# Six durations in the cost model that orders the expert and dense stage

## The chip, the cores and the metric
The kernel runs on one core of a Trainium2 chip. The metric is the device time of one execution in microseconds (us); the kernel before has a median of 881.43 us over 3 runs (877.85 to 882.18 us).

## The reference, cut to what matters
Three parts follow one another. Windowed attention with 32 global tokens gives 2176 tokens of 512 features. A router then assigns each token to exactly one of 8 experts, 272 tokens each, in falling order of the logits, and each expert computes two layers on its tokens. A dense layer with a rational activation closes.

```python
logits = x @ w_gate                       # x: attention's output, 2176 x 512
for idx in np.argsort(-logits.flatten()): # greedy, at most cap = 272 tokens per expert
    ...
for e in range(8):                        # 512 -> 1024 -> 512
    out[mask] = np.maximum(x[mask] @ w1[e], 0.0) @ w2[e]
h = out @ w_in                            # 512 -> 2048
P = a[0] + a[1]*h + a[2]*h**2 + a[3]*h**3
Q = 1.0 + abs(b[0])*abs(h) + abs(b[1])*h**2
y = (P / (Q + 1e-6)) @ w_out              # 2048 -> 512
```

## The kernel before, in words
Attention takes the first 190 us and is ordered by a planner of its own; the diff does not touch it. The stage after it, called the expert and dense stage here, runs on one planner object (`Flow`) with several generators that work side by side:

- `router` goes through 8 phases (`phase`, line 1188). Each but the last has a search (`search`, from line 988): 7 VectorE steps on a 136-element table, then six rounds of a wide comparison on VectorE (L1015), 17 small products on TensorE (L1019), a reduction (L1023), a broadcast product (L1027) and two or three narrow VectorE steps. `members` then turns the choice into token numbers (`idx`, L1167).
- `gather` fetches the tokens of an expert by three indirect DMAs from GpSimd (L1416), transposes them on TensorE (L1443) and splits each value into a high and a low part (L1428, L1430). Expert 0's gather waits for a staging slot (`t1_s`) that the conversions of the last dense weights also use.
- `loads` and `splits` bring expert weights in and split them: the high part on ScalarE (L1480), the low part by a subtraction on GpSimd (L1489; for every second piece of expert 0 on VectorE).
- `experts` has both layers of each expert: 64 groups of 3 products of 272 columns (`mm3`, L1244 to L1246), in which high and low parts are multiplied crosswise.
- `firsts` is the first dense layer, in chunks of two experts' blocks of 128 tokens (256 columns; the last chunk 384), again with `mm3`. After each bank of 512 (or 384) values comes `chain`, the activation: five ScalarE steps (L1620, L1622, L1627, L1641, L1643) and seven VectorE steps (L1638, L1630, L1632, L1654, L1656, L1658, L1660). L1654 and L1660 give the high and the low part of the result. One such bank with its chain is called a dense step below.
- `seconds` is the second dense layer, 3 products of 512 columns per group (`mm3t`, L1249 to L1251); the first two need the high part, the third the low part.
- `high`, `last_pieces`, `low_pe` and `low` finish the dense weights while the router's first searches run: conversions from 64-bit words on VectorE (L265 to L267), high parts on ScalarE (L1234), low parts by correction products on TensorE (L1355, L1356), by a copy on ScalarE (L1361), or on VectorE (L1379).

What sets the order is `Flow.run` (line 158 on). A generator yields the pair (engine, planned duration) before it issues instructions, and events, slots or rings before things it must wait for. The planner keeps a planned clock for each engine, adds a lag between dependent steps (0.2 us across engines, 0.14 us on VectorE), and takes at each turn, among the steps of an engine that could start within its patience, the one with the lowest rank. The engines' queues are then written in that order (`manual_schedule`), and at run time each engine goes through its queue in order, waiting on semaphores alone. The planned durations therefore never reach the chip. They set the order, and through `fill` (line 1719) how many filler products are put into planned gaps of TensorE before expert 0:

```python
t, e, d = min((max([self.free(e)] + [t + self.lag(s, e) for t, s in p[2]]) + sum(less), e, d)
              for e, d, *less in p[3])
...
wait = patience.get(e, 0.0)
x = min((x for x in c if x[0] <= t0 + wait), key=lambda x: (x[1], x[0]))
```

Ranks follow progress: `experts` has 2 + its share of experts done, `firsts` 2 + chunks done, `seconds` 0.1 less; `router` has 0 in its first two phases and later 0.6 or 1.5, and from its third phase on waits another `LAG` = 0.5 us of planned time before each TensorE step.

Of the kernel before, what the change touches and what calls it, by code (L numbers as in the profile page):

```python
# [188 lines left out]
def moe_kernel(ctx: ExitStack, tc: tile.TileContext, q_l, k_l, v_l, q_g, k_g, v_g, w_gate, w1, w2,  # L189
# [998 lines left out]
    def phase(j):  # L1188
        if j < E - 1:
            found = yield from search()  # L1190
        else:
            est = rw.tile([128, E], F32, name="est")
            yield "DVE", 0.3
            V.tensor_scalar(est, OPEN, 0.0, None, op0=OP.is_gt)
            found = *chosen(est), rps(128, 2 * E + 4 * NT)
        il = yield from members(j, *found, j == E - 1)
        yield from note(j, il)
# [80 lines left out]
    front = {"e": -1.0, "d": 0.0, "r": 0.0, "open": False}  # L1278

    def mmt(cols, n=1):  # L1280
        return n * cols / 2400

    def wide(n):
        return mo.tile([128, 512], F32, name=n, bufs={"rows": NR, "p": 2}[n])
# [99 lines left out]
    def router():  # L1384
        for j in range(E):
            if j >= 3:
                yield started[j - 3]
            for n, item in enumerate(phase(j)):
                front["r"] = j + n / 76
                if j > 1 and isinstance(item, tuple) and item[0] == "PE":  # L1390
                    yield LAG
                yield item
# [73 lines left out]
    def splits():  # L1466
        for j in range(E):
            for i in range(NX):
                alt = j == 0 and i % 2 == 1
                yield raw_done[j][i]  # L1470
                yield t2_s if alt else w_s
                yield "ACT", 0.52
                raw = raws.pop((j, i))
                if alt:
                    t = mo.tile([128, 2, 4, 128], F32R, name="t2", bufs=2)
                    hi, lo = t[:, 0], t[:, 1]
                else:
                    hi = mo.tile([128, 4, 128], F32R, name="whi", bufs=2)
                    lo = mo.tile([128, 4, 128], F32R, name="wlo", bufs=2)
                nc.scalar.activation(hi, raw, AF.Copy)  # L1480

                def rest(j, i, alt, raw, hi, lo):
                    if j < 2:
                        yield sought[j]
                    if alt:
                        yield "DVE", 0.6
                    else:
                        yield "POOL", 1.23
                    (V if alt else nc.gpsimd).tensor_tensor(lo, raw, hi.bitcast(F32), op=OP.subtract)  # L1489
                    wparts[j, i] = hi, lo, t2_s if alt else w_s  # L1490
                    flow.fire(w_done[j][i])
                    flow.fire(rows_s)

                flow.go(rest(j, i, alt, raw, hi, lo), -0.1)

    def experts():

        for j in range(E):
# [5 lines left out]
            for f in range(FC):  # L1504
                yield w_done[j][f]
                yield sc_s
                whi, wlo, slots = wparts.pop((j, f))
                ph = None
                for k in range(KC):
                    if f == 0:  # L1510
                        yield x_done[j][k]
                    yield "PE", mmt(CAP, 3)
                    if k == 0:
                        ph = four.pop(0)
                    mm3(ph[:, :CAP], whi[:, k], wlo[:, k], xhi[:, k], xlo[:, k], k == 0, k == KC - 1)
                    front["open"] = k < KC - 1
                    front["e"] = j - 1 + ER * (f + (k + 1) / KC) / NX
                flow.fire(slots)

                def act(j, f, ph, hs):  # L1520
                    yield "ACT", 0.28
                    hh = mo.tile([128, CAP], F32R, name="hh", bufs=FC)
                    hl = mo.tile([128, CAP], F32R, name="hl", bufs=FC)
                    nc.scalar.activation(hh, ph[:, :CAP], AF.Relu)  # L1524
                    yield "DVE", 0.35
                    V.scalar_tensor_tensor(hl, ph[:, :CAP], 0.0, hh.bitcast(F32), op0=OP.max, op1=OP.subtract)
                    hs[f] = hh, hl
                    four.append(ph)
                    flow.fire(sc_s)
                    flow.fire(h_done[j][f])  # L1530

                flow.go(act(j, f, ph, hs), -0.2)
            flow.fire(layer1[j])
            for d in range(KC):
                yield sc_s
                py = None
                for g in range(FC // 4):
                    i = FC + d * (FC // 4) + g
                    yield w_done[j][i]
                    whi, wlo, slots = wparts.pop((j, i))  # L1540
                    for c in range(4):
                        f = 4 * g + c
                        yield h_done[j][f]
                        yield "PE", mmt(CAP, 3)
                        if f == 0:
                            py = four.pop(0)
                        mm3(py[:, :CAP], whi[:, c], wlo[:, c], *hs[f], f == 0, f == FC - 1)
                        front["open"] = f < FC - 1
                        front["e"] = j - 1 + ER * (i + (c + 1) / 4) / NX
                    flow.fire(slots)  # L1550
# [22 lines left out]
    def shape(c):  # L1573
        T = 128 * len(BLK[c])
        return T, 512 // T
# [29 lines left out]
    def chain(c, i, ph):  # L1605
        T, FW = shape(c)
        big = FW > 1
        u = FW * T / 512
        own = big or i % 3 < 2
        hold = [t1_s] if own else [rows_s] * 3  # L1610
        for x in hold:
            yield x
        yield "ACT", 0.57 * u
        if own:
            t1 = mo.tile([128, 2, 512], F32, name="t1", bufs=2)
            p, q, r = wide("p"), t1[:, 0], t1[:, 1]
        else:
            p, q, r = [wide("rows") for _ in range(3)]
        p, q, r = [x[:, :FW * T] for x in (p, q, r)]
        nc.scalar.activation(q, ph, AF.Abs, scale=b0)  # L1620
        yield "ACT", 0.48 * u
        nc.scalar.activation(r, ph, AF.Square)  # L1622
        numer, quad = Event(), Event()

        def numerator():
            yield "ACT", 0.66 * u
            nc.scalar.activation(p, ph, AF.Identity, scale=a_[3], bias=a_[2])  # L1627
            yield quad
            yield "DVE", 0.6 * u
            V.tensor_tensor(p, p, ph, op=OP.mult)  # L1630
            yield "DVE", 0.66 * u
            V.scalar_tensor_tensor(p, p, a_[1], ph, op0=OP.add, op1=OP.mult)  # L1632
            flow.fire(numer)
            flow.fire(tq_s)

        flow.go(numerator(), 1)
        yield "DVE", 0.66 * u
        V.scalar_tensor_tensor(q, r, b1, q, op0=OP.mult, op1=OP.add)  # L1638
        flow.fire(quad)
        yield "ACT", 0.61 * u  # L1640
        nc.scalar.activation(r, q, AF.Ln, bias=cq)  # L1641
        yield "ACT", 0.52 * u
        nc.scalar.activation(r, r, AF.Exp, scale=-1.0)  # L1643
        yield numer
        slots = t2_s if big or i % 2 else w_s
        yield slots

        yield "DVE", 0.66 * u
        if slots is t2_s:
            t2 = mo.tile([128, 2, 512], F32R, name="t2", bufs=2)  # L1650
            gh, gl = t2[:, 0, :FW * T], t2[:, 1, :FW * T]
        else:
            gh, gl = [mo.tile([128, 512], F32R, name=n, bufs=2)[:, :FW * T] for n in ("whi", "wlo")]
        V.scalar_tensor_tensor(gh, p, a_[0], r, op0=OP.add, op1=OP.mult)  # L1654
        yield "DVE", 0.66 * u
        V.scalar_tensor_tensor(q, q, cq, gh.bitcast(F32), op0=OP.add, op1=OP.mult)  # L1656
        yield "DVE", 0.66 * u
        V.scalar_tensor_tensor(q, p, a_[0], q, op0=OP.add, op1=OP.subtract)  # L1658
        yield "DVE", 0.6 * u
        V.tensor_tensor(gl, q, r, op=OP.mult)  # L1660
        gs[c, i] = gh, gl, slots
        for x in hold:
            flow.fire(x)
        flow.fire(g_done[c][i])
# [108 lines left out]
```

## Time and profile before

| | before |
|---|---|
| median of 3 runs | 881.43 us (877.85 to 882.18) |
| profiled execution, its own time | 881.8 us |
| its span | 880.0 us |
| mean granted TensorE clock | 0.973 |
| TensorE busy | 830.7 us (94%), 7945 products |
| VectorE busy | 712.1 us (81%) |
| ScalarE busy | 504.1 us (57%) |
| GpSimd busy | 260.8 us (30%) |
| first product of expert 0 starts | 248.4 us |
| last product starts | 873.5 us |

How to read it: all times inside a trace count from the start of the span. Engines are PE (TensorE products), PEld (its weight loads, which run beside products), DVE (VectorE), ACT (ScalarE), POOL (GpSimd) and SP (SyncE, which issues DMAs). L1244 is line 1244 of the kernel. A product's duration includes time in which the next one already runs, since products are pipelined; the spacing of their starts is the better measure of pace. The granted clock is a share of full speed (1.00 is 2.4 GHz, half of it 1.2 GHz).

### The profile page before, as it was taken

The numbers are of one execution on the slowest core, as the hardware profiler recorded it, in microseconds if no ns is written. First come the engines' busy times: TensorE is split into PE (matmuls) and PEld (weight loads), VectorE is DVE, ScalarE is ACT, GpSimd is POOL, SyncE is SP. The second block draws the span as 40 slices with busy tenths as digits, with TensorE's granted clock in tenths as the row PEclk, the third lists the DMA queues.
The fourth block names the chain that finished last, engine by engine and source line by source line (L and its number), as shares of the span: only waits on it lengthen the run. The fifth ranks groups of instructions, "written<-read, shape, count | busy, mean of one in ns | idle before, by whom it ended". The sixth has DMA issues, their size and how long they took to land.

```text
span 880.0 us, 20528 instructions
## 1 busy us (share of the span) xinstructions
PE 830.7 (94%) x7945; PEld 730.3 (83%) x7956; DVE 712.1 (81%) x1647; ACT 504.1 (57%) x1137; POOL 260.8 (30%) x227
## 2 busy tenths in 40 slices
PE   8887988879899999999999999999999999999997
PEld 5665766657689899999889999998999999998995
DVE  4557777758889989989998989999887767668985
ACT  4665676759544545545554554555455555556753
POOL 7510220000223334233442433334243343330001
PEclk9998997989999999999999999999999999999999
DMA  9989885623444222221331222133223122210000
GB/s 218 243 237 271 207 254 160 181 77 97 141 123 122 73 60 62 73 85 37 97 97 48 73 75 83 37 97 98 60 61 107 50 73 84 85 37 13 13 1 36
DMA packets 130538, 88.99 MB, mean 101 GB/s; under 512 B 28840, under 2 KB 119464, under 8 KB 130440
## 3 DMA queue, kind: packets, MB, share of 16 engines
q1 hardware_dynamic: 126632, 76.92, 31.6%
q0 software_dynamic: 3280, 10.75, 3.7%
q8 instruction: 62, 1.02, 0.5%
q14 instruction: 36, 0.29, 0.1%
q10 hardware_dynamic: 528, 0.02, 0.0%
HBM read 70.02 MB, written 8.92 MB: 90 GB/s over the span
## 4 chain that ended last, share of the span: by engine, by line
PE 65%; DVE 14%; issue 10%; DMA 6%; ACT 3%; SPq 2%; POOL 1%; DVEq 0%; POOLq 0%; ACTq 0%
PE sc L1244 6%; PE sc L1246 6%; PE sc L1245 5%; PE sc L1251 5%; PE sc L1249 5%; PE sc L1250 5%; PE tq L1244 5%; PE tq L1245 5%; PE tq L1246 5%; PE sc L596 3%; DMA stg<-in_moe_w_out_dram 2%; SPq L383 2%; PE sc L494 2%; PE tq L1355 2%; PE av L1019 2%
## 5 line engine op out<-in xcount | busy, mean ns | idle before, releaser
L1489 POOL TENSOR_TENSOR wlo<-rows,whi 128x512 fp32r<-128x512 f32 x120 | 168.0, 1402 | 333.3 <-ACT whi L1480 324.7
L1244 PE MATMUL tq<-yr,wh 128*128 128x256 f32 (+1 forms) x512 | 148.4, 290 | 1.5 <-DVE p L1632 1.5
L1245 PE MATMUL tq<-yr,wh 128*128 128x256 f32 (+1 forms) x512 | 147.4, 288 | 0.0
L1246 PE MATMUL tq<-yr,ws 128*128 128x256 f32 (+1 forms) x512 | 146.9, 287 | 0.0
L1249 PE MATMUL sc<-wh,t 128*128 128x512 f32 x248 | 99.9, 403 | 0.0
L1251 PE MATMUL sc<-wh,t 128*128 128x512 f32 x248 | 99.0, 399 | 0.8 <-DVE t L1660 0.7
L1244 PEld LDWEIGHTS tq<-yr,wh 128*128 128x128 f32 x512 | 96.5, 188 | 3.1 <-issue 2.2
L1250 PE MATMUL sc<-ws,t 128*128 128x512 f32 x248 | 97.9, 395 | 0.0
L1245 PEld LDWEIGHTS tq<-yr,wh 128*128 128x128 f32 x512 | 96.4, 188 | 0.8
L1246 PEld LDWEIGHTS tq<-yr,ws 128*128 128x128 f32 x512 | 96.6, 189 | 0.0
L1480 ACT ACTIVATE whi<-rows 128x512 fp32r<-128x512 f32 x120 | 75.1, 628 | 17.0 <-PE sc L1245 13.1
L1620 ACT ACTIVATE t<-tq,coef 128x512 f32<-128x512 f32 (+1 forms) x67 | 44.9, 670 | 52.5 <-PE tq L1246 40.9
L1524 ACT ACTIVATE hh<-sc 128x272 fp32r<-128x272 f32 x64 | 25.4, 397 | 86.4 <-PE sc L1246 86.1
L1244 PE MATMUL sc<-xhi,whi 128*128 128x272 f32 x240 | 72.9, 304 | 0.0
L1244 PE MATMUL sc<-hh,whi 128*128 128x272 f32 x240 | 70.6, 294 | 0.0
L1246 PE MATMUL sc<-xhi,wlo 128*128 128x272 f32 x240 | 69.6, 290 | 0.5 <-POOL wlo L1489 0.5
L1246 PE MATMUL sc<-hh,wlo 128*128 128x272 f32 x240 | 69.3, 289 | 0.0
L1245 PE MATMUL sc<-hl,whi 128*128 128x272 f32 x240 | 69.2, 288 | 0.0
L1245 PE MATMUL sc<-xlo,whi 128*128 128x272 f32 x240 | 69.1, 288 | 0.0
L1638 DVE SCALAR_TENSOR_TENSOR t<-t,b 128x512 f32<-128x512 f32 (+1 forms) x67 | 52.0, 776 | 20.3 <-ACT t L1622 20.2
L1641 ACT ACTIVATE t<-t,cq 128x512 f32<-128x512 f32 (+1 forms) x67 | 47.3, 706 | 23.4 <-DVE t L1638 23.2
L1251 PEld LDWEIGHTS sc<-wh,t 128*128 128x128 f32 x248 | 46.6, 188 | 15.9 <-DVE t L1660 5.2
(313 smaller groups left out, 2182.2 us busy)
## 6 DMA issues: line engine op xcount, KB each, us to landing
rows<-in_moe_w_dram SPq DMA_DIRECT2D x128, 256.0 KB, 2.8
stg<-in_moe_w_in_dram SPq DMA_DIRECT2D x16, 512.0 KB, 4.3
stg<-in_moe_w_out_dram SPq DMA_DIRECT2D x16, 512.0 KB, 7.8
VW<-vr SPq DMA_DIRECT2D x18, 256.0 KB, 3.2
kr<-in_k_l_dram SPq DMA_DIRECT2D x8, 512.0 KB, 5.9
qr<-in_q_l_dram SPq DMA_DIRECT2D x8, 512.0 KB
vr<-in_v_l_dram SPq DMA_DIRECT2D x16, 256.0 KB, 5.3
xd<-xs SPq DMA_DIRECT2D x64, 64.0 KB, 3.3
```

The lines of the kernel that those rows point to most:

```text
L596: nc.tensor.matmul(ps[64 * j:64 * j + 64, n * 128:(n + 1) * 128], qb_t[u // 2][:, 2 * hg + j, u % 2 * 4 + n].rearrange("p a q -> p (a q)") ...
L1244: nc.tensor.matmul(ps, whi, xhi, start=first, stop=False)
L1245: nc.tensor.matmul(ps, whi, xlo, start=False, stop=False)
L1246: nc.tensor.matmul(ps, wlo, xhi, start=False, stop=last)
L1249: nc.tensor.matmul(ps, ghi, whi, start=first, stop=False)
L1250: nc.tensor.matmul(ps, ghi, wlo, start=False, stop=False)
L1251: nc.tensor.matmul(ps, glo, whi, start=False, stop=last)
L1480: nc.scalar.activation(hi, raw, AF.Copy)
L1489: (V if alt else nc.gpsimd).tensor_tensor(lo, raw, hi.bitcast(F32), op=OP.subtract)
L1620: nc.scalar.activation(q, ph, AF.Abs, scale=b0)
L1638: V.scalar_tensor_tensor(q, r, b1, q, op0=OP.mult, op1=OP.add)
L1641: nc.scalar.activation(r, q, AF.Ln, bias=cq)
```

## The change
Six kinds of planned durations get other values: `mmt`, which prices the products of `experts`, `firsts` and `seconds`; every VectorE step of `router` (0.05 us more); the GpSimd subtraction of an expert weight; and five VectorE steps of `chain`. No instruction, buffer, slot, rank or patience is edited.

```diff
--- before.py
+++ after.py
@@ -1278,7 +1278,7 @@
     front = {"e": -1.0, "d": 0.0, "r": 0.0, "open": False}
 
     def mmt(cols, n=1):
-        return n * cols / 2400
+        return n * (cols / 2260 + 0.005)
 
     def wide(n):
         return mo.tile([128, 512], F32, name=n, bufs={"rows": NR, "p": 2}[n])
@@ -1387,6 +1387,8 @@
                 yield started[j - 3]
             for n, item in enumerate(phase(j)):
                 front["r"] = j + n / 76
+                if isinstance(item, tuple) and item[0] == "DVE":
+                    item = ("DVE", item[1] + 0.05)
                 if j > 1 and isinstance(item, tuple) and item[0] == "PE":
                     yield LAG
                 yield item
@@ -1485,7 +1487,7 @@
                     if alt:
                         yield "DVE", 0.6
                     else:
-                        yield "POOL", 1.23
+                        yield "POOL", 1.4
                     (V if alt else nc.gpsimd).tensor_tensor(lo, raw, hi.bitcast(F32), op=OP.subtract)
                     wparts[j, i] = hi, lo, t2_s if alt else w_s
                     flow.fire(w_done[j][i])
@@ -1634,7 +1636,7 @@
             flow.fire(tq_s)
 
         flow.go(numerator(), 1)
-        yield "DVE", 0.66 * u
+        yield "DVE", 0.7 * u
         V.scalar_tensor_tensor(q, r, b1, q, op0=OP.mult, op1=OP.add)
         flow.fire(quad)
         yield "ACT", 0.61 * u
@@ -1645,18 +1647,18 @@
         slots = t2_s if big or i % 2 else w_s
         yield slots
 
-        yield "DVE", 0.66 * u
+        yield "DVE", 0.72 * u
         if slots is t2_s:
             t2 = mo.tile([128, 2, 512], F32R, name="t2", bufs=2)
             gh, gl = t2[:, 0, :FW * T], t2[:, 1, :FW * T]
         else:
             gh, gl = [mo.tile([128, 512], F32R, name=n, bufs=2)[:, :FW * T] for n in ("whi", "wlo")]
         V.scalar_tensor_tensor(gh, p, a_[0], r, op0=OP.add, op1=OP.mult)
-        yield "DVE", 0.66 * u
+        yield "DVE", 0.76 * u
         V.scalar_tensor_tensor(q, q, cq, gh.bitcast(F32), op0=OP.add, op1=OP.mult)
-        yield "DVE", 0.66 * u
+        yield "DVE", 0.72 * u
         V.scalar_tensor_tensor(q, p, a_[0], q, op0=OP.add, op1=OP.subtract)
-        yield "DVE", 0.6 * u
+        yield "DVE", 0.78 * u
         V.tensor_tensor(gl, q, r, op=OP.mult)
         gs[c, i] = gh, gl, slots
         for x in hold:
```

## Rows read from the trace of the kernel before

**Rows 1.** Stretches: busy us of each engine (instructions), granted clock, DMA share, GB/s.
```profile
230.00:240.00 10.00, 6.97 (x63) 5.24 (x62) 7.94 (x22) 3.53 (x6) 5.53 (x5) 0.91 0.37 108
240.00:249.00 9.00, 7.94 (x80) 6.26 (x80) 6.08 (x24) 2.67 (x6) 0.00 (x0) 0.72 0.50 147
...
600.00:650.00 50.00, 49.96 (x393) 45.82 (x392) 44.78 (x104) 25.19 (x46) 20.25 (x18) 1.00 0.20 61
650.00:700.00 50.00, 49.56 (x365) 46.18 (x364) 37.95 (x62) 27.89 (x52) 20.02 (x17) 1.00 0.32 93
```
**Rows 2.** Timeline, TensorE: start us, duration us, line, operation, out<-in, shape, count.
```profile
502.84 0.28 PE L1246 MATMUL tq<-yr,ws 128*128 128x256 f32 x1
...
504.25 0.28 PE L1246 MATMUL tq<-yr,ws 128*128 128x256 f32 x1
...
507.49 0.40 PE L1249 MATMUL sc<-wh,t 128*128 128x512 f32 x1
...
508.65 0.39 PE L1251 MATMUL sc<-wh,t 128*128 128x512 f32 x1
```
**Rows 3.** TensorE's waits, 262 to 640 us: us in total, times, longest.
```profile
PE av L1027 <- DVE d L1023: 1.3, 2, 0.9
...
PE sc L1246 <- POOL wlo L1489: 0.5, 3, 0.2
PE av L1063 <- DVE aa L1058: 0.4, 1, 0.4
```
**Rows 4.** TensorE's waits, 640 to 880 us.
```profile
PE tq L1244 <- DVE p L1632: 1.5, 1, 1.5
PE sc L1251 <- DVE t L1660: 0.7, 3, 0.3
PE tx L1443 <- DMA rows<-xd,idx: 0.4, 1, 0.4
```
**Rows 5.** Groups by line and shape, 262 to 875 us: busy us, mean ns, idle before.
```profile
L1489 POOL TENSOR_TENSOR wlo<-rows,whi 128x512 fp32r<-128x512 f32 x114 | 160.0, 1405 | 314.5 <-ACT whi L1480 305.9 <-issue 6.0 <-PE tq L1246 2.5
...
L1660 DVE TENSOR_TENSOR t<-t 128x512 fp32r<-128x512 f32 x56 | 53.2, 950 | 0.6
...
L1638 DVE SCALAR_TENSOR_TENSOR t<-t,b 128x512 f32<-128x512 f32 x56 | 45.3, 808 | 18.8 <-ACT t L1622 18.7
...
L1620 ACT ACTIVATE t<-tq,coef 128x512 f32<-128x512 f32 x56 | 38.5, 687 | 41.7 <-PE tq L1246 37.7 <-DVE d L1023 3.0 <-PE av L1027 0.7
```
**Rows 6.** Timeline, a dense step whose last product waits (in brackets: idle before, releaser).
```profile
727.88 1.67 DVE L1660 TENSOR_TENSOR t<-t 128x512 fp32r<-128x512 f32 x1
...
729.60 0.50 PE L1251 MATMUL sc<-wh,t 128*128 128x512 f32 x1 [0.34 <-DVE t L1660]
```
**Rows 7.** Timelines of the lead-in by engine, and the landing line of the gather.
```profile
219.52 0.42 DVE L265 TENSOR_SCALAR p<-stg 128x512 int32<-128x512 int32 x1
...
222.73 0.30 DVE L996 TENSOR_REDUCE m<-wide_b 128x17 f32<-128x136 f32 x1
...
234.69 3.08 DVE L265 TENSOR_SCALAR p<-stg 128x512 int32<-128x512 int32 x1
...
234.01 0.95 POOL L1416 DMA_INDIRECT p<-xd,idx  x1 [0.82 <-ACT ws L1361]
234.98 2.49 POOL L1489 TENSOR_TENSOR wlo<-rows,whi 128x512 fp32r<-128x512 f32 x2
...
DMA to landing us min/median/max: 3.2/3.5/4.2
...
238.70 0.21 PE L1027 MATMUL av<-identb,d 128*128 128x32 bf16 x1 [2.65 <-DVE d L1023]
...
241.90 0.58 PE L1019 MATMUL av<-oh,wide_a 128*128 128x8 bf16 x17
...
244.28 0.58 PE L1019 MATMUL av<-oh,wide_a 128*128 128x8 bf16 x17 [0.68 <-DVE wide_a L1015]
...
245.18 0.67 PE L1443 MATMUL tx<-identf,t 128*128 128x128 f32 x2
```

## The prediction, made before the changed kernel was run

> **What bounds the kernel now.** I read the slices of the span first, then busy time by stretches, then who waits for whom on TensorE, then the timeline where TensorE stops. From about 250 us to 873.5 us TensorE is busy in 99 to 100% of nearly every stretch, at the full granted clock, while VectorE has 44.8 of 50 us while the router runs and 38.0 of 50 us once it has ended, about 660 us [rows 1]. A busy TensorE is not yet a TensorE at its peak, so I checked the spacing of starts. Between the starts at 502.84 and 504.25 us lie 12 intervals of 256 columns, 0.1175 us each; between 507.49 and 508.65 us lie 5 of 512 columns, 0.232 us each [rows 2]. Back to back, then. The code has 512 groups of three for the experts (272 columns), 512 for the first dense layer (448 of them with 256 columns and 64 with 384) and 272 for the second (512). With 0.1175 and 0.232 us read directly, and 0.125 and 0.175 us for 272 and 384 columns as estimates on the line through these two, that is 158 + 34 + 192 + 189 = 573 us of 625 us. The rest is the router's small products, the transposes of gathered rows, weight loads that these leave uncovered, and waits. The waits that the profile names from 262 us on are few: four kinds before 640 us, from 1.3 down to 0.4 us and 3.0 us in all [rows 3], of which the first, the third and the last stand there, and three after it, 1.5, 0.7 and 0.4 us [rows 4]. So 5.6 us is all that a better order could take from named waits in this stage. The other place is the lead-in, 191 to 248 us, where the first search of the router is a chain between VectorE and TensorE and TensorE has real holes: 6.97 busy us of 10 and 7.94 of 9 in its last two stretches, at granted clocks of 0.91 and 0.72 [rows 1].
>
> **The change part by part.** No instruction is added, removed or resized. Six numbers change in a model that only decides in which order each engine's queue is written. The chip's durations are what they were, so the cost is that of other neighbours in five queues and of a few filler products.
>
> *Products, cols/2400 to cols/2260 + 0.005.* 256 columns go from 0.1067 to 0.1183 us and 512 from 0.2133 to 0.2315 us; the chip's 0.1175 and 0.232 us [rows 2] agree with the new ones. Over 1,253,376 columns in 3,888 products the plan grows from 522 to 574 us, the chip by 0. What goes with it is a hidden margin: for each 10 us that TensorE really worked, the old plan counted about 9.1 us, so whatever was planned just in time came 0.9 us early.
>
> *Activation chain.* The five repriced VectorE steps were planned at 4 x 0.66 + 0.60 = 3.24 us, are now at 0.70 + 0.72 + 0.76 + 0.72 + 0.78 = 3.68 us, and took 4.35 us on average, from 0.808 us for the first of the five to 0.950 us for the last [rows 5]. The five ScalarE steps keep prices below their means, the first 0.57 against 0.687 us [rows 5]. A chain's plan is about 7.5 us long, so it loses 0.09 x 7.5 = 0.7 us of margin by the new products and gets 0.44 us back: 0.25 us less per dense step. TensorE already takes some steps the moment they end: at 729.60 us the third product of a step waited for the subtraction that had started at 727.88 us and took 1.67 us [rows 6].
>
> *Router steps, +0.05 us.* One of them is planned at 0.21 us and took 0.30 us [rows 7]. Up to about 661 us some nine of them run inside one chain on the same engine, which gives back 0.4 us of plan: the 0.25 us above are covered there. After 661 us that cover is gone. Some 17 dense steps lie between there and the last chunk. The price lies between 0 (the margin is not used) and 17 x 0.25 = 4.3 us; I take +1.0 us, near the lower end, since such waits are 0.7 us in all [rows 4]. The last chunk, after 799 us, is out of it: its steps are made well ahead of their use, and its one wait is for another step (1.5 us at L1244) [rows 4].
>
> *GpSimd subtraction, 1.23 to 1.40 us.* Its mean is 1.405 us [rows 5]. GpSimd idles 314 us of this stage, and TensorE waits for it 0.5 us in all [rows 3]. Between -0.5 and +0.5 us; I take 0. With the longer last step of the chain (0.60 to 0.78 us) the 0.7 us that L1251 waits can go in part: -0.7 to 0, I take -0.3 us.
>
> *Lead-in.* The last gathered rows of expert 0 are issued by 234.96 us and rows land 3.5 us after their issue in the median [rows 7], here at about 238.5 us; their first transpose starts at 245.18 us, because it stands in TensorE's queue behind the rounds of the second search, one of which starts at 241.90 and the next at 244.28 us [rows 7]. Each round is planned 0.20 to 0.25 us longer now and the gather's own path is not, so the transposes may pass a round: one is worth 2.4 us. Against it, the gap of a round on VectorE in which a weight conversion fits (0.43 us of products and two lags) has no changed duration in it, so conversions, which release the gather, keep their places among the rounds; and a longer planned round can admit one more half of a weight-correction product (planned at 0.65 us), which holds up the search; by up to 0.5 us in each of six rounds, as I estimate from the holes of that size. Between -6 and +3 us; I take -1.0 us, close to no change.
>
> In that lead-in an integer step (L265) that takes 0.42 us elsewhere took 3.08 us from 234.69 us on, while two GpSimd subtractions ran for 2.49 us from 234.98 us; TensorE then waited 2.65 us [rows 7]. The Trainium skill, page "SBUF — State Buffer", section "Who interferes with whom", says that VectorE and GpSimd share one port pair as an exclusive lock, and that whichever starts first keeps the other out altogether. The trace agrees: the step took 3.08 us, to within 0.4 us of the end of both subtractions, and 0.42 us when nothing ran there [rows 7]. This speaks against the change: a mean over held and free instructions is the duration of neither, and a plan built on it does not know which pairs will meet. By means the 2.65 us would go and the lead-in be worth -3.6 us; by the lock that gain is luck, and the term stays where the rounds alone put it, at -1.0 us.
>
> **The sum.** 0 + 1.0 + 0 - 0.3 - 1.0 = -0.3 us. Against the profiled execution (881.8 us, span 880.0 us) that is 881.5 us; the median of the three runs shown, 881.43 us, lies 0.4 us below it, so the forecast is 881.1 us. The three runs spread over 4.3 us, so about 0.5%, 4.4 us, is what a measurement can tell from no change.
>
> **The rivals.**
> *The lead-in gets shorter (chance 0.30).* The conversion step and the subtractions no longer meet and the transposes pass one round. For it: the data lay there for 6.7 us. Against it: the lock has no price in the plan. Worth 2.65 us, some 1.0 us of the low clock that followed (0.72 of full speed [rows 1]), and 2.4 us: 6.0 us, 875.1 us.
> *Dense steps come late (0.22): the slower side.* With TensorE planned at its true speed and ScalarE still below its means, the second layer's products are put right behind chains that end later than planned; they wait at L1249 and L1251, and everything behind them in TensorE's queue waits too. For it: the wait at 729.60 us already exists, with the margin. Against it: only 0.7 us of it in total. If the 17 steps after 661 us each wait 0.5 us, that is 8.5 us, 889.6 us. It decides when more than nine of them wait so long.
> *The order hardly changes (inside the forecast, 0.05 of its 0.48).* If ranks and slots alone set the order, all five queues keep it and the time is 881.4 us.
>
> **How the numbers follow.** The forecast, between 877.0 and 885.8 us, gets 0.48. The faster case gets 0.30, below 877.0 us, and the slower one 0.22, above 885.8 us. The forecast's own terms span from -6.0 - 0.7 - 0.5 = -7.2 us to 4.3 + 3.0 + 0.5 = +7.8 us, 874 to 889 us; a little beyond it on both sides, 873 to 890 us, takes in both rivals' central times and leaves out two in ten, for the cases in which they go further.
>
> **What would show it.** Right: the same count of instructions on every engine, spacing of products unchanged, start of expert 0 within 2 us of 248.4 us, named TensorE waits after 262 us of 3 to 9 us in all, and the end of the last product within 4 us of 873.5 us. The faster rival: expert 0 starts at 243 us or before. The slower: L1249 and L1251 wait 5 us or more for L1654 and L1660 after 661 us. Wrong altogether: a new kind of wait, such as weights or gathered rows late for an expert in mid-stage, which nothing in these rows foretells.

## The result, and the profile after

The changed kernel takes 888.69 us (median; 886.78 to 891.70) against 880.55 us for the kernel before in the same comparison: a ratio of 1.0092, interval 1.0064 to 1.0119. It is slower by just under one per cent, where no change was forecast. Its profiled execution took 886.78 us with a span of 885.0 us, 5.0 us more than before, and 20,578 instructions instead of 20,528. 46 of the 50 are 23 more products on TensorE with their weight loads, all before expert 1: 5 are fillers, and 18 belong to three pieces of the last dense weights, whose low part the new plan leaves to TensorE (six correction products, L1355 and L1356, and a copy on ScalarE, L1361) instead of VectorE (L1379). So the planned durations also decide which engine does a step. The copies, before and after:

```profile
L1361 ACT ACTIVATE ws<-tq 128x512 fp32r<-128x512 f32 x28 | 16.6, 593 | 7.7 <-PE tq L1356 6.3 <-PE av L1027 1.3
...
L1361 ACT ACTIVATE ws<-tq 128x512 fp32r<-128x512 f32 x31 | 18.4, 594 | 11.9 <-PE av L1027 6.3 <-PE tq L1356 5.3
```

The stage is cut at five marks of the trace: the first VectorE step of the first search, then the first product of expert 0, of expert 1 and of expert 7, and the start of the last product. In us:

| kernel | search to expert 0 | expert 0 to 1 | expert 1 to 7 | expert 7 to last product | in all |
|---|---|---|---|---|---|
| before | 56.7 | 30.0 | 453.6 | 141.5 | 681.8 |
| after | 57.8 | 32.8 | 453.9 | 145.0 | 689.4 |
| difference | +1.1 | +2.8 | +0.3 | +3.5 | +7.6 |

Attention, which the diff does not touch, ended 2.6 us earlier in this execution (191.7 and 189.1 us; over all traces of this study 188.5 to 194.1 us), so the span shows 5.0 us of the 7.6. By these marks the loss lies at both ends of the stage and the long middle is as long as before. But the new order also moves products across the marks, so a longer stretch is not yet a wait; the lines below tell the two apart.

First, the stretches of the changed kernel, with the columns of [rows 1]. The last two lines cut the stretch from expert 7 on at the first product of the last chunk.

```profile
230.00:240.00 10.00, 6.99 (x63) 4.82 (x61) 6.72 (x17) 3.71 (x7) 5.54 (x5) 0.90 0.43 131
240.00:249.00 9.00, 8.11 (x87) 5.63 (x87) 7.03 (x24) 2.59 (x7) 0.00 (x0) 0.93 0.38 118
246.84:279.62 32.78, 30.11 (x284) 29.00 (x282) 28.43 (x75) 14.85 (x32) 13.34 (x11) 1.00 0.46 139
300.00:640.00 340.00, 337.77 (x2825) 307.80 (x2824) 314.08 (x686) 176.80 (x329) 130.15 (x99) 1.00 0.24 72
733.52:804.43 70.91, 70.49 (x488) 65.31 (x486) 49.87 (x68) 38.28 (x69) 24.13 (x20) 1.00 0.20 60
804.43:878.48 74.05, 70.65 (x349) 62.91 (x348) 63.77 (x119) 46.27 (x89) 2.34 (x5) 1.00 0.02 8
```

The same view of the kernel before, for stretches that [rows 1] do not have:

```profile
248.39:278.42 30.03, 28.29 (x257) 27.61 (x256) 27.64 (x69) 14.07 (x30) 13.59 (x11) 1.00 0.51 150
300.00:640.00 340.00, 338.86 (x2825) 310.31 (x2825) 312.27 (x693) 177.74 (x329) 123.42 (x99) 1.00 0.24 72
732.01:799.02 67.01, 66.83 (x469) 62.28 (x468) 46.21 (x66) 35.13 (x64) 22.59 (x20) 1.00 0.17 52
799.02:873.50 74.48, 72.96 (x361) 65.21 (x360) 64.14 (x120) 46.05 (x89) 2.40 (x5) 1.00 0.02 8
```

The length less TensorE's busy time (the first number after the length) is its idle time, the count behind it its products. Expert 0's stretch is 2.8 us longer with 27 more products and 0.9 us more idle. From expert 7 to the last chunk it is 3.9 us longer with 19 more products and only 0.2 us more idle; the last chunk is 0.4 us shorter with 12 fewer products and 1.9 us more idle. Over the whole stage TensorE's idle time went from 11.8 to 15.7 us, about half of the 7.6; the rest is busy time, with the 23 more products in it.

TensorE's waits of the changed kernel: from 262 to 640 us the first four lines, from 640 us on the last three (us in total, times, longest). They answer to [rows 3, 4].

```profile
PE av L1019 <- DVE wide_a L1015: 2.5, 5, 1.4
PE av L1150 <- DVE wide_a L1145: 1.3, 1, 1.3
PE sc L1251 <- DVE t L1662: 0.8, 4, 0.2
PE av L1063 <- DVE aa L1058: 0.4, 1, 0.4
...
PE tq L1244 <- DVE p L1634: 3.4, 3, 1.4
PE sc L1251 <- DVE t L1662: 0.9, 3, 0.3
PE sc L1246 <- POOL wlo L1491: 0.2, 1, 0.2
```

These are 9.5 us, against 5.6 us before (lines behind 1390 stand two further down now). The three that grew most are in two places, which the timeline of the changed kernel shows (start, duration, and in brackets the idle time before and who ended it):

```profile
233.61 3.59 DVE L1015 TENSOR_TENSOR wide_a<-m,nxt 128x544 bf16<-128x544 f32 x1
...
231.00 0.73 DVE L1015 TENSOR_TENSOR wide_a<-m,nxt 128x544 bf16<-128x544 f32 x1
...
234.10 2.50 POOL L1491 TENSOR_TENSOR wlo<-rows,whi 128x512 fp32r<-128x512 f32 x2
...
237.25 0.58 PE L1019 MATMUL av<-oh,wide_a 128*128 128x8 bf16 x17 [3.01 <-DVE wide_a L1015]
...
245.58 0.41 PE L1445 MATMUL tx<-identf,t 128*128 128x128 f32 x2
...
264.35 0.59 PE L1150 MATMUL av<-wide_a,wide_b 128*128 128x34 bf16 x17 [1.28 <-DVE wide_a L1145]
...
276.28 0.58 PE L1019 MATMUL av<-oh,wide_a 128*128 128x8 bf16 x17 [1.40 <-DVE wide_a L1015]
...
808.12 0.41 PE L1244 MATMUL tq<-yr,wh 128*128 128x384 f32 x1 [1.41 <-DVE p L1634]
811.48 0.41 PE L1244 MATMUL tq<-yr,wh 128*128 128x384 f32 x1 [1.00 <-DVE p L1634]
817.63 0.41 PE L1244 MATMUL tq<-yr,wh 128*128 128x384 f32 x1 [0.99 <-DVE p L1634]
```

In expert 0's stretch 1.28 + 1.40 = 2.7 us stand where the kernel before had 1.7 us:

```profile
PE av L1027 <- DVE d L1023: 0.9, 1, 0.9
PE av L1150 <- DVE wide_a L1145: 0.8, 1, 0.8
```

So 1.0 of its +2.8 us are waits. The other 1.8 us are busy time of TensorE, with 17 router products (L1063) and 6 dense products in it that stood elsewhere before.

In the last chunk the three waits are 3.4 us where one of 1.5 us stood [rows 4]. Their reason can be read from the order. In the kernel before, where the chunk starts at 799.02 us, three groups of the second layer stand between the chunk's first and second bank of products, and a fourth between the second and the third. The first and the fourth of them start here:

```profile
801.15 0.39 PE L1249 MATMUL sc<-wh,t 128*128 128x512 f32 x1
...
805.36 0.39 PE L1249 MATMUL sc<-wh,t 128*128 128x512 f32 x1
```

In the changed kernel none stands at these two places, and TensorE is idle there (808.12 and 811.48 us) until VectorE has read an earlier bank (L1634). Four groups more, 12 products, are done between expert 7 and the chunk instead (groups before and after):

```profile
L1249 PE MATMUL sc<-wh,t 128*128 128x512 f32 x28 | 11.1, 396 | 0.0
...
L1249 PE MATMUL sc<-wh,t 128*128 128x512 f32 x32 | 12.6, 395 | 0.0
```

All eight kernels of the table below with 12 products fewer in the last chunk (e1, e5, e6, e7, e9, e11, e16 and the kernel after) have 3.40 to 3.79 us of idle TensorE in it, the other twelve 0.95 to 2.14 us. The lead-in's lines belong to the paragraph on the lock below.

Groups by line and shape, 262 to 880 us:

```profile
L1491 POOL TENSOR_TENSOR wlo<-rows,whi 128x512 fp32r<-128x512 f32 x114 | 166.5, 1463 | 317.9 <-ACT whi L1482 260.1 <-PE sc L1246 45.7 <-PE tq L1246 7.5
...
L1249 PE MATMUL sc<-wh,t 128*128 128x512 f32 x248 | 100.1, 404 | 0.0
...
L1662 DVE TENSOR_TENSOR t<-t 128x512 fp32r<-128x512 f32 x56 | 48.6, 868 | 0.8
L1640 DVE SCALAR_TENSOR_TENSOR t<-t,b 128x512 f32<-128x512 f32 x56 | 45.3, 809 | 21.8 <-ACT t L1624 21.7
```

Set against [rows 5], the last step of the activation chain now takes 868 ns instead of 950 and the GpSimd subtraction 1,463 instead of 1,405. The median of that chain step is 691 ns in both traces: the mean moves with the few instructions that are held up. What a "measured duration" measures so depends itself on which instructions meet, and on the order.

### The profile page after: what moved, and what is told of

Same layout as the page of the kernel before. It is cut to its first block, busy times and chain, and to the rows that moved or that the text cites. A ratio compares the mean times of both kernels' runs of the same rounds, so it can differ in the third digit from the quotient of the medians.

```text
span 885.0 us, 20578 instructions
## 1 busy us (share of the span) xinstructions
PE 833.2 (94%) x7968; PEld 729.1 (82%) x7979; DVE 715.9 (81%) x1644; ACT 504.0 (57%) x1140; POOL 268.1 (30%) x227
## 3 DMA queue, kind: packets, MB, share of 16 engines
q8 instruction: 62, 1.02, 0.5%
## 4 chain that ended last, share of the span: by engine, by line
PE 64%; DVE 15%; issue 9%; DMA 5%; ACT 4%; SPq 1%; POOL 1%; POOLq 0%; DVEq 0%; ACTq 0%
PE sc L1251 5%; PE sc L1244 5%; PE sc L1246 5%; PE sc L1245 5%; PE sc L1249 5%; PE sc L1250 5%; PE tq L1244 5%; PE tq L1245 5%; PE tq L1246 5%; PE sc L596 3%; DMA stg<-in_moe_w_out_dram 2%; PE tq L1355 2%; DVE wide_a L1015 2%; PE sc L494 2%; PE tq L627 2%
## 5 line engine op out<-in xcount | busy, mean ns | idle before, releaser
L1491 POOL TENSOR_TENSOR wlo<-rows,whi 128x512 fp32r<-128x512 f32 x120 | 174.2, 1454 | 337.1 <-ACT whi L1482 279.2
L1251 PE MATMUL sc<-wh,t 128*128 128x512 f32 x248 | 99.6, 401 | 1.9 <-DVE t L1662 1.7
L1249 PE MATMUL sc<-wh,t 128*128 128x512 f32 x248 | 100.1, 404 | 0.0
L1251 PEld LDWEIGHTS sc<-wh,t 128*128 128x128 f32 x248 | 46.5, 188 | 19.2 <-DVE t L1662 8.8
```

The source lines that it names most:

```text
L1249: nc.tensor.matmul(ps, ghi, whi, start=first, stop=False)
L1251: nc.tensor.matmul(ps, glo, whi, start=False, stop=last)
```

## The experiments

The first four take the change apart; the others were made because these four did not add up. For each kernel the table gives the stretches between the marks as above, the ratio to the kernel before with its interval, and one number from the code, the **planned share**: the sum of all durations that the planner gives to VectorE between its own times for the start of expert 1 and of expert 7, divided by the planned time between these two. On the chip VectorE was busy 0.889 of that stretch in the kernel before. The stretches are those of one execution per kernel, which can lie 4.4 us from the kernel's median (e12 above it, e14 below). Five kernels have one and the same order of TensorE up to expert 1 (before, e3, e11, e12, e13), and their first two stretches are 55.5 to 56.7 and 30.0 to 31.4 us: differences of that size are no effect of an order.

| kernel | planned share | to exp. 0 | 0 to 1 | 1 to 7 | 7 to last | ratio |
|---|---|---|---|---|---|---|
| e10 | .690 | 53.5 | 36.5 | 476.7 | 144.9 | 1.0332 [1.0299, 1.0365] |
| e8 | .702 | 56.7 | 33.1 | 471.7 | 144.4 | 1.0279 [1.0257, 1.0300] |
| e1 | .709 | 55.8 | 32.2 | 479.1 | 148.1 | 1.0384 [1.0350, 1.0417] |
| e5 | .742 | 58.6 | 32.8 | 476.2 | 151.1 | 1.0425 [1.0403, 1.0447] |
| e6 | .746 | 55.6 | 31.1 | 478.3 | 146.1 | 1.0342 [1.0315, 1.0370] |
| e13 | .770 | 56.3 | 31.3 | 459.3 | 141.1 | 1.0043 [1.0023, 1.0064] |
| e14 | .775 | 53.4 | 32.9 | 459.6 | 141.4 | 1.0082 [1.0055, 1.0109] |
| **before** | .776 | 56.7 | 30.0 | 453.6 | 141.5 | 1 |
| e9 | .777 | 61.2 | 29.9 | 462.4 | 146.4 | 1.0190 [1.0159, 1.0222] |
| e18 | .779 | 56.4 | 32.9 | 457.1 | 139.6 | 1.0048 [1.0029, 1.0066] |
| e7 | .788 | 56.2 | 32.8 | 455.8 | 145.2 | 1.0143 [1.0112, 1.0174] |
| e16 | .790 | 58.0 | 36.3 | 459.2 | 145.6 | 1.0175 [1.0149, 1.0200] |
| **after** | .791 | 57.8 | 32.8 | 453.9 | 145.0 | 1.0092 [1.0064, 1.0119] |
| e11 | .792 | 55.5 | 30.0 | 459.1 | 145.2 | 1.0118 [1.0090, 1.0147] |
| e15 | .797 | 58.7 | 30.0 | 456.9 | 142.2 | 1.0062 [1.0038, 1.0086] |
| e2 | .808 | 59.0 | 33.8 | 459.8 | 141.3 | 1.0140 [1.0115, 1.0165] |
| e3 | .823 | 56.4 | 31.3 | 452.9 | 141.8 | 1.0005 [0.9989, 1.0021] |
| e4 | .846 | 59.0 | 33.8 | 459.4 | 142.1 | 1.0133 [1.0105, 1.0161] |
| e12 | .846 | 56.5 | 31.4 | 453.8 | 146.6 | 1.0044 [1.0021, 1.0067] |
| e17 | .857 | 58.7 | 32.1 | 455.2 | 144.5 | 1.0104 [1.0081, 1.0127] |

**The change in parts.** e1 has the new price of the products alone, e2 the router's +0.05 us alone, e3 the five prices of the chain alone, e4 all but the products' price. The edit of e1 is

```diff
-        return n * cols / 2400
+        return n * (cols / 2260 + 0.005)
```

and those of the other three are the remaining hunks of the change.

> Only the price of products changes (cols/2260 + 0.005); router, GpSimd and chain keep their old prices. Margin theory (a TensorE that the plan believes 9% too fast hides 0.9 us per 10 us, and the new price takes it away): this alone carries the loss, ratio 1.006 to 1.012 against the kernel before, with L1244 waiting for the numerator 3 us or more in the last chunk. Router theory (the loss comes from the 0.05 us of the router steps, by way of the lead-in and the second search): ratio 0.997 to 1.003. Order-luck theory (any new order differs by some us, parts don't add): anything from 0.995 to 1.010, and e1 to e3 don't add up to the whole.

> Only the router's VectorE steps are 0.05 us longer in the plan. Margin theory: 0.997 to 1.003, since it gives margin to nothing but the router. Router theory: 1.006 to 1.012, with expert 1's first product more than 2 us later after expert 0's than in the kernel before (30.0 us there). Order-luck theory: 0.995 to 1.010.

> Only the five VectorE steps of the activation chain are longer in the plan (0.44 us in all for 512 columns). Margin theory: more margin for each dense step, so 0.995 to 1.001, and fewer waits of L1251 than 0.7 us after 640 us. Router theory: 0.997 to 1.003. Order-luck theory: 0.995 to 1.010.

> The whole change without the price of products. Margin theory: at or below the kernel before, 0.994 to 1.002, since margin is only added. Router theory: 1.006 to 1.012. Order-luck theory: 0.995 to 1.010, and not the sum of e2 and e3.

No theory's ranges hold all four: e1 lies above all three, e2 and e4 just above the router theory's 1.012, e3 within all. The chain's prices cost nothing (e3). The router's alone cost 1.4%, and e4, which has them too, nearly the same (1.3%). The products' price alone, the one that agrees with the chip to within 1%, costs 3.8%, four times the whole change. Its stretch, its chain by engine and its waits, 300 to 640 us:

```profile
300.00:640.00 340.00, 323.01 (x2675) 291.20 (x2674) 306.56 (x643) 169.37 (x316) 119.73 (x95) 0.99 0.23 69
```
```profile
PE 47%; DVE 29%; issue 11%; ACT 7%; DMA 4%; SPq 1%; POOL 1%; DVEq 0%; POOLq 0%; ACTq 0%
```
```profile
PE av L1027 <- DVE d L1023: 7.6, 6, 1.6
PE sc L1251 <- DVE t L1660: 4.5, 10, 1.1
PE sc L1251 <- DVE il L1155: 1.6, 2, 0.8
PE av L1019 <- DVE wide_a L1015: 1.4, 2, 0.7
```

TensorE is idle for 17.0 of 340 us, 1.1 us in the kernel before, and VectorE holds 29% of the chain that ended last. The line of the kernel before:

```profile
PE 65%; DVE 14%; issue 10%; DMA 6%; ACT 3%; SPq 2%; POOL 1%; DVEq 0%; POOLq 0%; ACTq 0%
```

The longest of the waits, in e1's timeline of VectorE, GpSimd and TensorE:

```profile
464.91 0.79 DVE L1654 SCALAR_TENSOR_TENSOR t<-p,coef,t 128x512 fp32r<-128x512 f32 x1
465.74 3.36 DVE L1656 SCALAR_TENSOR_TENSOR t<-t,cq,t 128x512 f32<-128x512 f32 x1
469.02 0.43 DVE L1526 SCALAR_TENSOR_TENSOR hl<-sc,hh 128x272 fp32r<-128x272 f32 x1
469.37 0.15 DVE L1023 CUSTOM_DVE_ANT_0 junk<-av,REM 128x8 f32<-128x8 f32 x1
...
466.02 2.52 POOL L1489 TENSOR_TENSOR wlo<-rows,whi 128x512 fp32r<-128x512 f32 x2
...
469.59 0.19 PE L1027 MATMUL av<-identb,d 128*128 128x32 bf16 x1 [1.61 <-DVE d L1023]
```

A short router step (L1023), whose result TensorE needs at once, stands in VectorE's queue behind a chain step that two GpSimd subtractions hold for 3.36 us. The same product waits 1.50 to 1.61 us at 386.75, 469.59, 551.02 and 633.77 us, 81 to 83 us apart, with the same lines in the same order before it: the plan repeats itself, and a place of that kind in the order is paid for with four experts here. These four waits are 6.1 of the 17.0 us.

**Which of the other prices makes up for the products'?** e5 adds the router's to e1's, e6 the chain's and GpSimd's. e8 tests my first theory, a lost margin in time: it adds 0.7 us to the planned lag from VectorE or ScalarE to TensorE on top of e1, from expert 1's first product on (`front["e"]` is below 0 until then, so not from expert 0 on, as the expectation below has it).

```diff
+        more = 0.7 if dst == "PE" and src in ("DVE", "ACT") and self.late() else 0.0
-        return self.SAME.get(src, 0.0) if src == dst else 0.2
+        return self.SAME.get(src, 0.0) if src == dst else 0.2 + more
...
+    flow.late = lambda: front["e"] >= 0
```

> New price of products and 0.05 us on every router step; chain and GpSimd keep their old prices. Margin theory (products alone cost 35 us because router steps and dense steps lose the time that a too fast planned TensorE hid; the router's 0.05 us gives the router its part back): ratio 1.008 to 1.018, with L1027 waiting under 2 us for L1023 between 262 and 640 us (7.6 us with products alone) but L1251 still waiting for the chain. Rival (the chain's new prices are what rescues the whole change): 1.03 or more.

> The whole change without the router's 0.05 us. Margin theory: the router's steps stay short of margin, L1027 waits 5 us or more for L1023 between 262 and 640 us; ratio 1.02 to 1.035. Rival (the chain's prices are the rescue): 1.005 to 1.012, like the whole change.

> New price of products alone, and from expert 0 on a planned lag of 0.9 instead of 0.2 us from VectorE and ScalarE to TensorE, which is the hidden margin said openly. Margin theory: most of the 35 us of products alone come back, ratio 0.998 to 1.012, L1027 and L1251 waiting under 3 us each after 262 us. Rival (the price of products hurts by the balance of ranks and engines, not by late operands): 1.025 or more.

Neither part alone brings the middle back (476.2 and 478.3 us); both together, which is the changed kernel, do (453.9). e5 went the rival's way. e6's ratio lies where the margin theory had put it, but not for its reason: L1027 waits 1.6 us there for L1023 (262 to 640 us), not 5. In e8 (300 to 640 us) that wait falls from e1's 7.6 us to 1.7 us and L1251's for the chain from 4.5 to 2.6 us, as the theory asked, but TensorE's wait for the router's wide step (L1015) grows from 1.4 to 4.9 us, and the explicit margin returns only about a quarter of e1's loss. A margin at TensorE's operands is thus a small part of what was missing at most, and that theory fell.

**The balance of two prices.** What e1 changes beside durations is how busy the plan believes VectorE to be, relative to TensorE: 0.709 of the time, where it is 0.889 on the chip. e10 therefore reprices no product and makes all VectorE steps cheaper by a tenth; e9 leaves e1's products and makes VectorE dearer by a tenth; e12 makes it dearer by a tenth in the kernel before, from expert 1's first product on.

```diff
-                p[3] = item if isinstance(item, list) else [item]
+                p[3] = [(e, d * self.scale.get(e, 1.0), *m) for e, d, *m in (item if isinstance(item, list) else [item])]
...
+    flow.scale = {"DVE": 0.9}
```

> The kernel before with every planned VectorE duration of the stage times 0.9 and the old price of products; the planned share of VectorE falls from 0.776 to 0.69. Balance theory: 1.02 to 1.045, though no product is repriced, with TensorE busy 330 us or less of 340 between 300 and 640 us. Rival (the price of products itself does the harm): 0.995 to 1.01.

> New price of products alone, and every planned VectorE duration of the expert and dense stage times 1.1 (ScalarE, GpSimd and lags stay). Balance theory: what counts is how much of TensorE's planned time the planned VectorE work fills. From expert 1 to expert 7 that share is 0.776 in the plan of the kernel before and 0.791 in the changed one, and 0.71 to 0.75 in the three slow mixtures (products alone, with the router, with chain and GpSimd); here it is 0.777. So ratio 1.000 to 1.014, VectorE over 310 of 340 us busy between 300 and 640 us. Rival (the particular steps that the change reprices must have their margin): 1.02 or more.

> The kernel before with every planned VectorE duration times 1.1 from expert 1's first product on; the planned share rises to 0.846. Balance theory with a knee near 0.76: nothing is lost and little is to be gained, 0.994 to 1.003, named TensorE waits after 300 us at most 5 us. Rival (the optimum is where the kernel before lies, and both sides of it lose): 1.006 or more.

e10 reproduces e1 without touching a product: +3.3%, and a middle of 476.7 us. Its stretch from 300 to 640 us and its waits there (lines one further down):

```profile
300.00:640.00 340.00, 322.30 (x2653) 291.15 (x2652) 296.42 (x641) 165.06 (x310) 115.35 (x94) 0.98 0.22 67
```
```profile
PE av L1020 <- DVE wide_a L1016: 6.9, 7, 2.6
PE sc L1252 <- DVE t L1661: 4.8, 10, 1.1
```

TensorE is busy 322.3 us of 340, as in e1 (323.0), and again waits for a router step and for the last step of the chain. The stretch in e9:

```profile
300.00:640.00 340.00, 333.80 (x2785) 302.36 (x2784) 311.26 (x674) 174.52 (x326) 123.19 (x98) 1.00 0.24 70
```

e9 takes back 16.7 of the 25.5 us that e1 lost in the middle, but with a worse lead-in (61.2 us) only half of its 3.8%, less than I had expected and just short of the rival's 1.02. In the table the middle is 472 to 479 us in all five kernels with a planned share up to .746, and 453 to 462 us in all fifteen from .770 on; between them there is no gradual slope in these runs, and why the step lies there stays open. That the share itself is the cause is not shown: a new price of VectorE changes the planned length of its chains as well, and no run parts the two. Above the step more share buys nothing: e12 at .846 has the middle of the kernel before and costs 0.44% in all, a little more than I had allowed and less than the rival asked (its profiled execution shows 5.1 us behind expert 7, but was 4.4 us above its median); its named waits after 300 us, 7.0 us, miss the 5 us that I had allowed.

**The remaining 0.9%.** e7 is the changed kernel with the router's +0.05 us only from its third phase on, to give back the lead-in; e11 has the new prices only between expert 1's first product and the last chunk, to give back both ends.

```diff
-                if isinstance(item, tuple) and item[0] == "DVE":
+                if j > 1 and isinstance(item, tuple) and item[0] == "DVE":
                     item = ("DVE", item[1] + 0.05)
```
```diff
+    def new():
+        return front["e"] >= 0 and front["d"] < E - 1
```

> The whole change, but the router's 0.05 us from its third phase on alone. If the router's price costs in the lead-in (router steps alone: first product of expert 1 comes 92.8 us after the first search starts, 86.7 us before) and gives back later: ratio 1.001 to 1.006, first product of expert 1 within 88 us of the first search. Rival (the lead-in is noise of the order, or the two first phases need the margin as well): 1.009 or more.

> The whole change, but its new prices hold only from expert 1's first product to the begin of the last dense chunk; lead-in and last chunk are planned at the old prices (planned share in between 0.792). If what is left of the loss sits at the two ends (the stretch from the first search to expert 1's first product, 86.7 us before and 90.5 after, and the last chunk, 74.5 and 74.1 us but with 3.4 us of waits): 0.997 to 1.004. Rival (it sits in the middle): 1.006 to 1.012.

Both missed, and both fell where their rivals had put them. The router's 0.05 us does cost in the lead-in: the seven kernels that have it in the first two phases (e2, e4, e5, e15, e16, e17 and the kernel after) take 57.8 to 59.0 us to expert 0, the ten that leave the first two phases at the old prices 55.5 to 56.7 us. So e7 shortens the lead-in to 56.2 us, but still loses 2.8 us in expert 0's stretch and 3.7 us in the last; e11 has the order of the kernel before up to expert 1 (55.5 and 30.0 us) and loses 5.5 us in the middle, which was as long as before in the kernel after, and 3.7 us in the last stretch. The loss is not tied to one place: each new order has its own.

So the last runs ask how much any small repricing moves the time. Against the kernel before, e13 has `cols / 2390`, e18 `cols / 2410`, e14 +0.002 us on the router's VectorE steps. Against the kernel after, e15 has `cols / 2270`, e16 `cols / 2250`, e17 VectorE dearer by a tenth.

> The kernel before with the price of products at cols/2390 instead of cols/2400 (0.4%), nothing else; about a sixth of the planned TensorE steps change places. If the order of the kernel before is one draw among many of equal prices (draw theory): between 0.998 and 1.012, and with e14 not both within 0.002 of 1. If its order is what such prices give (price theory): 0.998 to 1.002.

> The kernel before with 0.002 us more on each planned VectorE step of the router (about 1%); a sixth of the planned TensorE steps change places. Draw theory: 0.998 to 1.012, above 1.003 in e13 or here. Price theory: 0.998 to 1.002.

> The kernel before with cols/2410 instead of cols/2400, a third neighbour. Draw theory: 0.998 to 1.012, and a mean of the three neighbours (1.0043, 1.0082 and this) above 1.003. Price theory: 0.998 to 1.002.

> The changed kernel with cols/2270 instead of cols/2260 in the price of products. Draw theory: away from the changed kernel's 1.009 by up to 0.006 on either side, and overlapping with e13 and e14. Price theory: 1.006 to 1.012, clear of e13 and e14.

> The changed kernel with cols/2250 instead of cols/2260. Draw theory: 1.003 to 1.015. Price theory: 1.006 to 1.012.

> The changed kernel with every planned VectorE duration of the stage times 1.1; the planned VectorE share goes from 0.791 to 0.857. Balance theory: no loss from the share, so between 1.000 and 1.015 as a draw, TensorE busy 334 us or more of 340 between 300 and 640 us. Rival (both directions away from 0.78 lose): above 1.018.

Three edits of prices by about 1% or less, in both directions, cost 0.43, 0.82 and 0.48% against the kernel before; no interval reaches the price theory's 1.002. Around the kernel after, 0.4% more or less on one price gives ratios of 1.0062 and 1.0175, the second outside both theories' ranges. e17, at a share of .857, takes 1.0104 with a middle of 455.2 us, so a large share does no harm there either, though TensorE is busy 333.1 us of 340 where I had asked for 334. The kernel before is thus the best or nearly so of its neighbours: of 19 other orders none was faster, one equal (e3). So a new order as such cost 0.4 to 0.8% in all three neighbours of the kernel before, though it need not cost anything (e3). 1.0092 [1.0064, 1.0119] is a little above the largest of the three, with overlapping intervals, and between the two neighbours of the kernel after: the new prices as such are neither shown to help nor to harm. That the kernel before stands out because its order was picked among many is an inference; no run here shows how it came about.

## Why the prediction was wrong

The sum of the terms was -0.3 us; the medians lie 8.1 us apart the other way.

**The lead-in, -1.0 us: wrong, and cut too short.** Expert 0 began 57.8 us after the first search step instead of 56.7, so this term was +1.1, and the table shows its sign to be that of the router's price: with the longer planned rounds the lead-in took more time, and no transpose passed a round. The sum stopped at expert 0's first product; the stretch behind it is 2.8 us longer (1.4 to 2.8 us against the five runs with the order of before), of which 1.0 us are waits, now for two wide VectorE steps of the router (L1145 and L1015) at 264.35 and 276.28 us. That the granted clock of the lead-in's last stretch was now 0.93 instead of 0.72 [rows 1] did not make up for it. The sum had no term for expert 0's own stretch.

**"The last chunk is out of it": the step that failed most.** From expert 7 on +3.5 us came, the largest piece, and the largest growth of TensorE's idle time in it, 1.9 us, is in the last chunk. I had concluded from a single wait of 1.5 us [rows 4] that the chains of the last chunk lie well ahead of their use. But that wait was for a bank that VectorE had not yet read, and the second layer's products were what hid more of the kind: with 12 of them moved ahead of the chunk the same wait stands three times, 3.4 us in all. One wait in one execution showed that this place was tight, and I read it as the place being safe. The chunk itself did not get longer (74.5 and 74.1 us), since the 12 products are done before it; of the 3.5 us, 2.1 are idle time, 0.7 are 6 products that stood in the middle before (0.1175 us each [rows 2]), and the last 0.7 have no name.

**"No instruction is added, removed or resized": wrong.** Three weight pieces changed from VectorE to TensorE and ScalarE, 18 products and 3 copies more. The lead-in's term had allowed for more such products, at up to 3 us, but I took the other side of its range. What the 18 cost by themselves is not shown.

**Dense steps after 661 us, +1.0 us: the net was near, the terms were not.** The middle moved by +0.3 us, with 12 fewer products in it and 0.9 us more idle time of TensorE. This is a difference of large numbers: the products' price alone costs 25.5 us there (e1), and the other prices return it. I had set the two sides at 0.7 and 0.44 us per step, as latencies of one chain. e10 has e1's loss without a product's price being changed, and in e8 a latency of 0.7 us given back heals little of it, so the planned load of VectorE beside that of TensorE fits the runs better than latency at TensorE does.

**Products 0, GpSimd 0: right in what the chip does.** The second layer's products take 404 ns in the records, 403 before, and TensorE's named waits for GpSimd after 262 us are 0.2 us, 0.5 before [rows 3]. L1251 did not lose its 0.7 us: it waits 0.8 + 0.9 us now, against the -0.3 that I took.

**The lock: right in kind.** L265 no longer met the subtractions, and that gave nothing, because the router's wide comparison did: 3.59 us instead of 0.73, with two subtractions running for 2.50 us from 234.10 us on, and TensorE waited 3.01 us for it instead of 2.65 [rows 7]. Expert 0's transposes again came behind the last round, at 245.58 us (245.18 before, with a first search that had started 2.6 us later). By the records L1015 had started 0.49 us before the subtractions and was the one held, as L1656 was in e1 and L265 in [rows 7], which the prediction passed over when it called the trace in agreement. These are the exceptions, though: of 57 VectorE steps in the trace of the kernel before that took over 0.8 us more than the median of their line and shape, a subtraction had begun first in 48, the step in 4, and none ran beside the other 5. The Trainium skill, page "SBUF — State Buffer", section "Who interferes with whom", which I had cited, gives the shared ports to whoever issues first. The trace agrees with it in that one of the two is held; on the order it can't decide, since the records show starts and not issues.

**The slower rival: its size nearly, its place not.** It foretold waits of 5 us or more at L1249 and L1251 for the chain's last steps after 661 us; they are 0.9 us. That its 889.6 us lie near the measured 888.69 us is luck. The case on the slower side that happened has no single place. Of my signs, the start of expert 0 held (189.1 + 57.8 = 246.9 us, with attention ending earlier); the named waits (9.5 us, for 3 to 9), the last product (878.5 us, 5.0 late where 4 were allowed) and the count of instructions missed narrowly.

**What was missing altogether** is the question of what any reordering does here. I treated a shuffle as worth nothing on average and gave "no change" the largest chance. In e13, e14 and e18 a shuffle near this order cost 0.4 to 0.8%.

## What to carry to other kernels

Where planned durations set the order of several engines' queues, test a new price together with the others that stay: one price made right beside others that stay too low cost 3.8% here, where the whole set cost 0.9%. The plan then held VectorE busy 0.709 of the time, where it was 0.889 on the chip. Judge such an edit against two or three meaningless ones of the same size: 0.4% on one price moved the kernel before by half as much as the whole edit did (0.43 and 0.48%), and the kernel after by 0.8% (e16). When a stretch gets longer, count the instructions in it before looking for a wait. And read a wait of one or two microseconds at a tight place as a warning for the next order, not as the bound on what that place can cost.

## What the runs showed of the hardware

A VectorE step that meets two GpSimd subtractions can take four to seven times as long; three kinds showed it: 3.08 us for 0.42 (an integer step [rows 7]), 3.59 for 0.73 (a comparison), 3.36 us where L1654 just before it took 0.79 (a chain step, e1). How much of this an order has does not decide its time alone: in the middle of e1 VectorE lost 61.8 us to steps more than 0.5 us above the median of their line and shape, 48.8 us in the kernel before, but 67.8 us in e12, whose middle is as short as before.
